# Token lists, gathers and weight chunks of a capacity-limited mixture of experts: moved token lists, moved gathers, a fourth raw buffer

## The chip, the cores and the metric

The kernel runs on one core of one Trainium2 chip, as one launch. The metric is the device time of one execution in microseconds (us). Engines are named as in the profile: PE (TensorE, matrix products), PEld (its weight loads), DVE (VectorE), ACT (ScalarE), POOL (GpSimd) and SP (SyncE, which here only issues DMAs).

## The reference, cut to what matters

```python
x = attention(q, k, v)                    # 4 batches, 8 heads, 576 positions; local and strided masks
x = x.reshape(2304, 512)
h = x @ w_in; x = maximum(0.01 * h, h) @ w_out          # 512 -> 2048 -> 512
logits = x @ w_gate                                     # 2304 tokens, 8 experts
order = argsort(-logits.flatten())
for idx in order:                                       # greedy: best pairs first
    tok, e = idx // 8, idx % 8
    if assigned[tok] >= 0 or counts[e] >= 288: continue
    assigned[tok] = e; counts[e] += 1
for e in range(8):                                      # 288 tokens each
    mask = assigned == e
    out[mask] = maximum(x[mask] @ w1[e], 0) @ w2[e]     # 512 -> 1024 -> 512
```

## The kernel before, in words

The program has three stages. Attention and most of the two-layer network `w_in`, `w_out` come first; the last two of six token blocks of that network have their second product done in `second(4)` and `second(5)` (lines 887 to 904), which write the tokens `x` to a DRAM buffer `x2d`. The change begins there. Then come the eight experts, in the order in which they fill up.

**Finding the experts.** `routes()` (lines 906 to 909) is a generator that goes round eight times. Round k has `search()`, which finds the next expert to be full and its threshold by five counting rounds: DVE builds 0/1 tiles `G` by comparisons, PE counts with them (`cnt`), DVE makes a flag, PE sums it (`tot`), and each needs the one before. `route(k)` then writes the number of the expert (`EXP[k]`, tile `ei`), a running count of its tokens by a scan and two small products (`po`), and strikes the chosen tokens and the expert out of the table `L`, `unl`, `opn`. `tokens(k)` turns the running count `s` into the list of the expert's 288 tokens: ten small DVE operations, three comparisons `OQ`, two tiles `rhs`, 18 products `pi`, and the list `idx` as whole numbers (`IDX[k]`). Only after that does the next search begin in the order of the program. `m`, `s`, `cc` and the other small state lie in one PSUM tile, `st`. DVE operations of this part are called through `soon` (line 641), which places them 2000 positions earlier in the planner's order.

**One expert.** `weights(k)` reads `EXP[k]` on SP and loads the expert's weights in eight chunks of 512 KB into three buffers `raw`: chunks 0 to 3 are `w1`, 4 to 7 are `w2`. ACT rounds each to `whi`; the rest `wlo = raw - whi` is taken by DVE for chunks 1, 5, 7 and by POOL for the other five; then the `raw` buffer is free again. There are two sets of `w1` tiles, but five buffers for the four chunks of `w2`, so that chunks 5 to 7 of the next expert can be rounded only when the last products of the running one have let go of theirs. `gather(k)` fetches the expert's tokens from `x2d` by three indirect DMAs that POOL issues, into one of two buffers `xg`; PE transposes them (`pet`), ACT and DVE write them as `exh` and `exl`. `expert(k)` has 96 products of 288 columns to the hidden layer, with ACT's `hh` and DVE's `hl` after each group, and 96 to the output (`g`, line 859 to 861); PE transposes the result (`pot`), ACT copies it into `o` (two buffers), and three indirect DMAs of POOL scatter it. The last quarter and the scatter of an expert are put off (`left_`) into the second column of the next one.

**What sets the order.** The main loop (lines 934 to 951) interleaves these generators: `expert(k)` yields 32 times; at every second yield `routes()` makes a step; at the yield with number 3 `need(k + 1)` runs `routes()` until the next token list is there, and `weights(k + 1)` begins, a chunk at each even yield from 6 to 20; `gather(k + 1)` follows at yields 22 to 24. One round of `routes()` has 16 steps, ten in the search, two in `route`, four in `tokens`, and an expert gives 16. So route(k + 2) runs beside expert k.

Each engine executes its own instructions strictly in order. That order is fixed when the program is built: a list planner with its own estimates of durations takes, for each engine, the ready instruction that stands first in the program; `tc.high_priority(n)` moves instructions n positions forward. On the chip an instruction waits by semaphores for what it needs, and all behind it on its engine wait too.

Of the kernel before, what the change touches and what calls it, by code (L numbers as in the profile page):

```python
# [7 lines left out]
F32 = mybir.dt.float32  # L8
# [5 lines left out]
OP = mybir.AluOpType  # L14
# [4 lines left out]
DM, FF = 512, 2048  # L19
# [7 lines left out]
def body(ctx, tc, q, k, v, w_in, w_out, w_gate, w1, w2, out):  # L27
    nc = tc.nc
    consts = ctx.enter_context(tc.tile_pool(name="consts", bufs=1, reuse_waits="tile"))
    dram = ctx.enter_context(tc.tile_pool(name="dram", bufs=1, space=bass.MemoryType.DRAM))  # L30
    x2d = dram.tile([NT, DM], F32, name="x2d")
# [443 lines left out]
    for n, _ in enumerate(mlp()):  # L475
        st = n // 7
# [47 lines left out]
    for n in range(64, 96):  # L524
# [22 lines left out]
        if f % 4 == 0:  # L547
            x = "hl"[f // 4 % 2]
# [8 lines left out]
        if f % 4 == 2 and f > 3 or f == 15:  # L557
            c = f // 4 - (f < 15)
# [69 lines left out]
    def rtile(shape, name, dt=F32, bufs=2):  # L628
        return rt.tile(shape, dt, name=name, tag=name, bufs=bufs)
# [5 lines left out]
    IDX, EXP = {}, {}  # L635
# [76 lines left out]
    def route(k):  # L712
        if k < 7:
            ab = yield from search()
        else:
            ab = rtile([128, 2, 18], "ab")
            soon.tensor_copy(ab[:, 0], unl)
            soon.memset(ab[:, 1], 0.0)
            soon.tensor_copy(oh, opn)
        ev = rtile([128, 1], "ev")  # L720
        t8 = rtile([128, 8], "t8")
        soon.scalar_tensor_tensor(t8, oh, 1.0, jf[:, :8], op0=OP.mult, op1=OP.mult, accum_out=ev)
        EXP[k] = rtile([128, 1], "ei", I32, bufs=8)
        soon.tensor_copy(EXP[k], ev)

        soon.tensor_tensor_scan(sc.rearrange("p a i -> p (a i)"), rst.rearrange("p a i -> p (a i)"),
                                     ab.rearrange("p a i -> p (a i)"), 0.0, op0=OP.mult, op1=OP.add)
        tot = rtile([128, 2], "tot", BF)
        soon.tensor_copy(tot, sc[:, :, 17])
        for _ in range(2):  # L730
            yield
        po = rbank([128, 2], "po")
        nc.tensor.matmul(po, tri, tot, start=True, stop=False)
        nc.tensor.matmul(po[:, 1:2], onesb, tot[:, 0:1], start=False, stop=True)
        s1 = rtile([128, 18], "s1")
        soon.scalar_tensor_tensor(s1, sc[:, 1], po[:, 1:2], ab[:, 1], op0=OP.add, op1=OP.mult)
        soon.scalar_tensor_tensor(s, sc[:, 0], po[:, 0:1], ab[:, 0], op0=OP.add, op1=OP.mult)
        soon.tensor_add(s, s, s1)
        if k < 7:
            t = rtile([128, 18], "t18")  # L740
            soon.tensor_scalar(t, s, 0.5, None, op0=OP.is_ge)
            soon.scalar_tensor_tensor(sel, s, 288.5, t, op0=OP.is_le, op1=OP.mult)
            soon.scalar_tensor_tensor(L, bc(sel, 8), -1.0e38, L, op0=OP.mult, op1=OP.add)
            soon.scalar_tensor_tensor(L, bc8(oh), -1.0e38, L, op0=OP.mult, op1=OP.add)
            soon.tensor_sub(unl, unl, sel)
            soon.tensor_sub(opn, opn, oh)
        yield from tokens(k)

    def tokens(k):

        c1 = rtile([128, 2, 18], "c1")
        soon.tensor_scalar(c1[:, 0], s, 96.5, None, op0=OP.is_ge)
        soon.tensor_scalar(c1[:, 1], s, 192.5, None, op0=OP.is_ge)
        soon.scalar_tensor_tensor(s, c1[:, 0], -96.0, s, op0=OP.mult, op1=OP.add)
        soon.scalar_tensor_tensor(s, c1[:, 1], -96.0, s, op0=OP.mult, op1=OP.add)
        soon.tensor_scalar(cc[:, 0], c1[:, 0], -1.0, 1.0, op0=OP.mult, op1=OP.add)
        soon.tensor_copy(cc[:, 2], c1[:, 1])
        soon.tensor_sub(cc[:, 1], c1[:, 0], cc[:, 2])
        soon.tensor_scalar(s, s, -1.0, None, op0=OP.add)
        OQ = rtile([128, 18, 96], "OQ", BF, bufs=1)  # L760
        for i in range(0, 18, 6):
            soon.tensor_tensor(OQ[:, i:i + 6], jf[:, None, :96].to_broadcast([128, 6, 96]),
                               s[:, i:i + 6].unsqueeze(2).to_broadcast([128, 6, 96]), op=OP.is_equal)
        rhs = rtile([128, 2, 3, 18], "rhs", BF)
        soon.tensor_mul(rhs[:, 0], cc, jf[:, None, :18].to_broadcast([128, 3, 18]))
        soon.tensor_scalar(rhs[:, 1], cc, tokp, None, op0=OP.mult)
        for _ in range(4):
            yield
        pi = rbank([96, 2, 3], "pi")
        for i in range(18):  # L770
            nc.tensor.matmul(pi.rearrange("p t c -> p (t c)"), OQ[:, i], rhs[:, :, :, i].rearrange("p t c -> p (t c)"),
                             start=(i == 0), stop=(i == 17))
        ip = rtile([96, 2, 3], "ip")
        soon.tensor_copy(ip, pi)
        IDX[k] = rtile([96, 3], "idx", I32, bufs=8)
        soon.scalar_tensor_tensor(IDX[k], ip[:, 0], 128.0, ip[:, 1], op0=OP.mult, op1=OP.add)
# [3 lines left out]
    def ind(ap):  # L780
        return bass.IndirectOffsetOnAxis(ap=ap, axis=0)

    def weights(k):
        e = nc.values_load(EXP[k][0:1, 0:1], engines=[mybir.EngineType.SP], min_val=0, max_val=7)
        W[k] = []
        for n in range(8):
            raw = POOLA[0].tile([128, 1024], F32, name="raw", tag="raw", bufs=3)
            if n < 4:
                nc.sync.dma_start(raw, w1[bass.ds(e, 1), 128 * n:128 * n + 128, :].rearrange("e p m -> (e p) m"))
            else:  # L790
                nc.sync.dma_start(raw.rearrange("p (j m) -> p j m", j=2),
                                  w2[bass.ds(e, 1), 256 * (n - 4):256 * (n - 4) + 256, :].rearrange(
                                      "e (j p) m -> p (e j) m", j=2))
            if n < 4 and k % 2:
                hi, lo = (xa.tile([128, 1024], F32R, name="w" + x, tag=f"WI{n + y}") for x, y in (("hi", 0), ("lo", 4)))
            else:
                pool, tag, bufs = (POOLB[0], "w2", 5) if n >= 4 else (POOLA[0], "w1", 4)
                hi = pool.tile([128, 1024], F32R, name="whi", tag=tag + "h", bufs=bufs)
                lo = pool.tile([128, 1024], F32R, name="wlo", tag=tag + "l", bufs=bufs)
            nc.scalar.activation(hi, raw, AF.Copy)  # L800
            (nc.vector if n in (1, 5, 7) else nc.gpsimd).tensor_sub(lo, raw, hi.bitcast(F32))  # L801
            W[k].append((hi, lo))
            yield

    def gather(k):
        xg = xa.tile([96, 3, DM], F32, name="xg", tag=("xh2", "xl2")[k % 2])
        for c in range(3):
            with tc.high_priority(2000):
                nc.gpsimd.indirect_dma_start(out=xg[:, c], out_offset=None, in_=x2d[:, :],
                                             in_offset=ind(IDX[k][:, c:c + 1]))  # L810
        if k % 2:
            xh, xl = (xa.tile([128, 4, 288], F32R, name="ex" + x, tag=f"x{x}3") for x in "hl")
        else:
# [13 lines left out]
    def expert(k):  # L827
# [4 lines left out]
        for j in range(8):  # L832
# [9 lines left out]
                left_.pop()()  # L842
            nc.scalar.activation(hh[:, j], p, AF.Relu)  # L843
            nc.vector.scalar_tensor_tensor(hl[:, j], p, 0.0, hh[:, j].bitcast(F32), op0=OP.max, op1=OP.subtract)
        o = e2.tile([96, 3, DM], F32, name="o", tag="o", bufs=2)

        def back(c, ot):
            pt = bank([96, 3, 128], "pot", "m")
# [19 lines left out]

        def end():
            back(3, ots[3])  # L870
            put()

        def put():
            for r in range(3):
                st = nc.gpsimd.indirect_dma_start(out=out, out_offset=ind(IDX[k][:, r:r + 1]), in_=o[:, r],
                                                  in_offset=None)
                for x in scat:
                    tc.declare_no_dep(st.ins, x.ins, reason="each token has one expert and one place")
                scat.append(st)
        if k < 7:  # L880
            left_.append(end)
        else:
# [21 lines left out]
            yield  # L904

    def routes():
        for k in range(8):
            yield from route(k)
            ROUTED[0] = k + 1

    ROUTED = [0]
    R = routes()

    def need(k):
        while ROUTED[0] <= k:
            next(R, None)

    for _ in second(4):
        next(R, None)
    gdx.close()  # L920
    POOLA[0] = ctx.enter_context(tc.tile_pool(name="pa", bufs=1, reuse_waits="tile"))
    need(0)
    wx = weights(0)
    for f, _ in enumerate(second(5)):
        next(R, None)
# [1 line left out]
            next(wx)  # L927
    right.close()
    POOLB[0] = ctx.enter_context(tc.tile_pool(name="pbx", bufs=1, reuse_waits="tile", side="right"))
    for _ in gather(0):  # L930
        pass
    for _ in wx:
        pass
    for k in range(8):
        nxt = iter(())
        for n, _ in enumerate(expert(k)):
            if n % 2 == 0:
                next(R, None)
            if n == 3 and k < 7:
                need(k + 1)  # L940
                wx = weights(k + 1)
            if n >= 6 and n % 2 == 0:
                next(wx, None)
            if n == 22 and k < 7:
                nxt = gather(k + 1)
                next(nxt)
            if n >= 22:
                next(nxt, None)
        for x in (wx, nxt):
            for _ in x:  # L950
                pass

# [29 lines left out]
```

## Time and profile before

| | |
|---|---|
| median of 3 runs | 925.15 us (921.23 to 933.21) |
| the profiled execution | 926.83 us |
| its span, first to last instruction | 925.1 us |
| mean granted TensorE clock | 0.963 |
| PE busy, share of the span | 860.2 us, 93% |
| DVE, ACT, POOL busy | 563.3, 441.9, 471.5 us |
| first product of expert 0, start of its last | 627.7 and 662.6 us |
| starts of experts 1 to 7 | 662.9, 697.1, 734.7, 773.1, 815.0, 856.6, 885.6 us |

Times within an execution are counted from the span's start. An instruction of PE is pipelined: one of 288 columns shows as 0.29 us busy, while the next begins 0.13 us after it, so that a wait on PE shows as a gap only when it is longer than the overlap.

### The profile page before, as it was taken

Reading aid. Unit: us, or ns where it says so; the run is one execution under the profiler, and the core shown is the slowest. Engines: PE = TensorE matmul, PEld = TensorE weight load, DVE = VectorE, ACT = ScalarE, POOL = GpSimd, SP = SyncE. Lnnn points to the kernel's source line nnn. Section 1 sums busy time; section 2 is a strip of 40 time slices with the busy share of each in tenths; the row PEclk is TensorE's granted clock in tenths of the full one; section 3 lists DMA queues with packets and bytes.
Section 4 is the critical chain, followed back from the end, with each engine's and each line's share of the span. In section 5 each row is a group of like instructions: output and inputs, shape, how many; then the busy total and the mean of one; then the engine's idle time right before and its main releaser. Section 6 shows DMA issues by size and latency. Waiting matters only on the chain.

```text
span 925.1 us, 16905 instructions
## 1 busy us (share of the span) xinstructions
PE 860.2 (93%) x6274; PEld 726.1 (78%) x6274; DVE 563.3 (61%) x1543; ACT 441.9 (48%) x1095; POOL 471.5 (51%) x394
## 2 busy tenths in 40 slices
PE   7889998899999999999999999978998989897994
PEld 4777766587887888778898877658998989797994
DVE  6777889856446445554555556566877767675330
ACT  5778667464446445454455423324435434243531
POOL 3645646564555556555655445745446263426621
PEclk9789999999999999999999999987999999798997
DMA  8596554320111100100000002325356362425710
GB/s 183 142 200 157 141 144 124 119 61 5 36 26 53 43 14 2 47 1 1 35 1 1 1 1 80 114 67 177 129 154 185 102 182 95 141 92 154 213 35 26
DMA packets 86450, 80.59 MB, mean 87 GB/s; under 512 B 65376, under 2 KB 65376, under 8 KB 86368
## 3 DMA queue, kind: packets, MB, share of 16 engines
q1 hardware_dynamic: 78688, 53.30, 21.1%
q0 software_dynamic: 7680, 26.22, 9.3%
q8 instruction: 49, 0.80, 0.4%
q14 instruction: 33, 0.27, 0.1%
HBM read 70.06 MB, written 9.44 MB: 86 GB/s over the span
## 4 chain that ended last, share of the span: by engine, by line
PE 64%; DMA 10%; DVE 9%; issue 7%; POOL 4%; ACT 4%; SPq 1%; POOLq 0%; ACTq 0%; DVEq 0%
PE p L373 5%; PE p L397 5%; DMA raw<-in_moe_w_dram 4%; PE p L375 4%; PE p L374 4%; PE p L399 4%; PE p L398 4%; PE g L859 3%; PE g L860 3%; PE g L861 3%; PE p L536 2%; PE q L896 2%; PE p L538 2%; PE pS L166 2%; PE p L537 2%
## 5 line engine op out<-in xcount | busy, mean ns | idle before, releaser
L352 POOL TENSOR_TENSOR lo<-WO,hi 128x512 fp32r<-128x512 f32 x96 | 126.6, 1319 | 95.1 <-ACT hi L349 94.9
L352 POOL TENSOR_TENSOR lo<-WI,hi 128x512 fp32r<-128x512 f32 x96 | 126.9, 1323 | 90.1 <-DVE hi L351 58.3
L801 POOL TENSOR_TENSOR wlo<-raw,whi 128x1024 fp32r<-128x1024 f32 x40 | 95.8, 2410 | 113.9 <-ACT whi L800 113.3
L373 PE MATMUL p<-xh,hi 128*128 128x384 f32 x256 | 98.1, 383 | 5.5 <-DVE g L382 5.5
L349 ACT ACTIVATE hi<-WO 128x512 fp32r<-128x512 f32 x96 | 60.5, 630 | 88.2 <-PE q L898 43.7
L375 PE MATMUL p<-xh,lo 128*128 128x384 f32 x256 | 86.9, 339 | 1.4 <-POOL lo L352 1.4
L800 ACT ACTIVATE whi<-raw 128x1024 fp32r<-128x1024 f32 x64 | 66.1, 1055 | 44.4 <-DMA raw<-in_moe_w_dram 39.2
L374 PE MATMUL p<-xl,hi 128*128 128x384 f32 x256 | 86.6, 338 | 0.6 <-DVE xl L234 0.6
L397 PE MATMUL p<-hi,gh 128*128 128x512 f32 x192 | 82.8, 431 | 0.8 <-ACT gh L383 0.8
L859 PE MATMUL g<-hh,whi 128*128 128x288 f32 x256 | 81.4, 319 | 0.5 <-ACT hh L843 0.5
L860 PE MATMUL g<-hl,whi 128*128 128x288 f32 x256 | 79.0, 309 | 0.1
L861 PE MATMUL g<-hh,wlo 128*128 128x288 f32 x256 | 78.7, 307 | 0.0
L836 PE MATMUL g<-exh,whi 128*128 128x288 f32 x256 | 78.4, 307 | 0.0
L837 PE MATMUL g<-exl,whi 128*128 128x288 f32 x256 | 77.4, 303 | 0.0
L838 PE MATMUL g<-exh,wlo 128*128 128x288 f32 x256 | 77.2, 302 | 0.0
L399 PE MATMUL p<-hi,gl 128*128 128x512 f32 x192 | 75.7, 394 | 1.3 <-DVE gl L384 1.3
L159 ACT ACTIVATE sc<-sc,mx 96x128 f32<-96x128 f32 (+2 forms) x176 | 67.6, 386 | 16.6 <-DVE mx L157 16.6
L398 PE MATMUL p<-lo,gh 128*128 128x512 f32 x192 | 75.2, 392 | 0.0
L373 PEld LDWEIGHTS p<-xh,hi 128*128 128x128 f32 x256 | 48.2, 188 | 16.6 <-DVE g L382 6.8
L181 POOL TENSOR_TENSOR sc<-sc,mx 96x384 f32<-96x384 f32 (+2 forms) x64 | 52.3, 834 | 17.3 <-DVE mx L179 10.2
L381 ACT ACTIVATE g<-p 128x384 f32<-128x384 f32 x64 | 31.1, 486 | 57.0 <-PE p L375 56.7
L351 DVE CAST hi<-WI 128x512 fp32r<-128x512 f32 x59 | 26.8, 454 | 46.1 <-PE p L374 35.9
(203 smaller groups left out, 2257.5 us busy)
## 6 DMA issues: line engine op xcount, KB each, us to landing
raw<-in_moe_w_dram SPq DMA_DIRECT2D x64, 512.0 KB
wraw<-in_moe_w_in_dram POOLq DMA_DIRECT2D x16, 512.0 KB
wraw<-in_moe_w_out_dram POOLq DMA_DIRECT2D x16, 512.0 KB
rawq<-in_q_dram SPq DMA_DIRECT2D x32, 144.0 KB
rawk<-in_k_dram SPq DMA_DIRECT2D x32, 144.0 KB
x2d<-x SPq DMA_DIRECT2D x18, 256.0 KB
vt<-in_v_dram SPq DMA_DIRECT2D x16, 160.0 KB
vt<-in_v_dram SPq DMA_DIRECT2D x48, 27.0 KB
```

The costliest lines, as they stand in the source:

```text
L352: nc.gpsimd.tensor_sub(lo, src, hi.bitcast(F32))
L373: nc.tensor.matmul(p1, wh[:, cs], xh[:, c], start=(c == 0), stop=False)
L374: nc.tensor.matmul(p1, wh[:, cs], xl[:, c], start=False, stop=False)
L375: nc.tensor.matmul(p1, wl[:, cs], xh[:, c], start=False, stop=(c == 3))
L397: nc.tensor.matmul(p2[t], gh[:, s], oh, start=(f == 0), stop=False)
L398: nc.tensor.matmul(p2[t], gh[:, s], ol, start=False, stop=False)
L399: nc.tensor.matmul(p2[t], gl[:, s], oh, start=False, stop=(f == 15))
L801: (nc.vector if n in (1, 5, 7) else nc.gpsimd).tensor_sub(lo, raw, hi.bitcast(F32))
L836: nc.tensor.matmul(p, wh, xh[:, c], start=(c == 0), stop=False)
L859: nc.tensor.matmul(p, wh, hh[:, j], start=(j == 0), stop=False)
L860: nc.tensor.matmul(p, wh, hl[:, j], start=False, stop=False)
L861: nc.tensor.matmul(p, wl, hh[:, j], start=False, stop=(j == 7))
```

## The change

- `route(k)` no longer runs `tokens(k)`. `routes()` keeps it as a generator `T` and makes one of its steps (seven now: the small operations, `OQ` and `rhs` are spread over them) beside each step of the search of round k + 1. Two counters, `FOUND` (the expert's number is known) and `LISTED` (its token list is there), take the place of `ROUTED`. A round of `routes()` has 12 steps then instead of 16, still 16 to an expert.
- `weights`: four `raw` buffers, not three; `wlo` of chunk 1 on POOL as well, so that six of eight are POOL's. `o` has one buffer, not two.
- The main loop waits for `FOUND` at yield 3, makes chunks 0 to 4 at yields 4 to 12, waits for `LISTED` at yield 16, issues the three gathers there, transposes at yields 24, 26, 28 and 30, and makes chunks 5 to 7 after the expert's last yield.
- The indirect DMAs of `gather` lose their `high_priority(2000)`, except that all of `gather(0)`, transposes included, gets 4000.

```diff
-        yield from tokens(k)
 
     def tokens(k):
...
+        yield
         soon.scalar_tensor_tensor(s, c1[:, 1], -96.0, s, op0=OP.mult, op1=OP.add)
+        soon.tensor_scalar(s, s, -1.0, None, op0=OP.add)
         soon.tensor_scalar(cc[:, 0], c1[:, 0], -1.0, 1.0, op0=OP.mult, op1=OP.add)
         soon.tensor_copy(cc[:, 2], c1[:, 1])
-        soon.tensor_sub(cc[:, 1], c1[:, 0], cc[:, 2])
-        soon.tensor_scalar(s, s, -1.0, None, op0=OP.add)
+        yield
...
         for i in range(0, 18, 6):
             soon.tensor_tensor(OQ[:, i:i + 6], ...)
+            yield
+        soon.tensor_sub(cc[:, 1], c1[:, 0], cc[:, 2])
...
-        for _ in range(4):
-            yield
+        yield
         pi = rbank([96, 2, 3], "pi")
...
+        yield
         ip = rtile([96, 2, 3], "ip")
...
-            raw = POOLA[0].tile([128, 1024], F32, name="raw", tag="raw", bufs=3)
+            raw = POOLA[0].tile([128, 1024], F32, name="raw", tag="raw", bufs=4)
...
-            (nc.vector if n in (1, 5, 7) else nc.gpsimd).tensor_sub(lo, raw, hi.bitcast(F32))
+            (nc.vector if n in (5, 7) else nc.gpsimd).tensor_sub(lo, raw, hi.bitcast(F32))
...
         for c in range(3):
-            with tc.high_priority(2000):
-                nc.gpsimd.indirect_dma_start(out=xg[:, c], ...)
+            nc.gpsimd.indirect_dma_start(out=xg[:, c], ...)
+        yield
...
-        o = e2.tile([96, 3, DM], F32, name="o", tag="o", bufs=2)
+        o = e2.tile([96, 3, DM], F32, name="o", tag="o")
...
     def routes():
+        T = iter(())
         for k in range(8):
-            yield from route(k)
-            ROUTED[0] = k + 1
+            if k == 7:
+                for _ in T:
+                    yield
+            for _ in route(k):
+                if k and next(T, 1) == 1:
+                    LISTED[0] = k
+                yield
+            for _ in T:
+                yield
+            LISTED[0] = k
+            FOUND[0] = k + 1
+            T = tokens(k)
+        for _ in T:
+            yield
+        LISTED[0] = 8
...
-    for _ in gather(0):
-        pass
+    need(LISTED, 0)
+    with tc.high_priority(4000):
+        for _ in gather(0):
+            pass
...
-            if n == 3 and k < 7:
-                need(k + 1)
-                wx = weights(k + 1)
-            if n >= 6 and n % 2 == 0:
-                next(wx, None)
-            if n == 22 and k < 7:
-                nxt = gather(k + 1)
-                next(nxt)
-            if n >= 22:
-                next(nxt, None)
-        for x in (wx, nxt):
+            if k < 7:
+                if n == 3:
+                    need(FOUND, k + 1)
+                    wx = weights(k + 1)
+                if 4 <= n < 14 and n % 2 == 0:
+                    next(wx)
+                if n == 16:
+                    need(LISTED, k + 1)
+                    nxt = gather(k + 1)
+                    next(nxt)
+                if n >= 24 and n % 2 == 0:
+                    next(nxt, None)
+        for x in (nxt, wx):
```

## Rows read from the trace of the kernel before

**Rows 1.** Windows by expert: length; PE, PEld, DVE, ACT, POOL busy; clock; DMA.

```profile
628.00:663.00 35.00, 34.46 (x292) 33.38 (x291) 25.82 (x70) 15.81 (x29) 13.25 (x6) 0.90 0.44 136
663.00:697.00 34.00, 33.17 (x315) 31.26 (x314) 25.84 (x68) 14.69 (x28) 17.55 (x12) 1.00 0.50 159
697.00:734.70 37.70, 34.60 (x337) 32.62 (x334) 27.97 (x69) 15.88 (x29) 17.69 (x12) 1.00 0.48 144
734.70:773.00 38.30, 35.45 (x332) 33.59 (x330) 27.24 (x68) 16.01 (x29) 18.52 (x12) 0.96 0.48 142
773.00:815.00 42.00, 37.30 (x307) 35.29 (x304) 27.77 (x74) 15.90 (x28) 17.21 (x12) 0.88 0.40 130
815.00:856.50 41.50, 34.86 (x288) 33.45 (x286) 27.52 (x85) 15.14 (x28) 19.58 (x15) 0.92 0.47 141
856.50:885.50 29.00, 28.42 (x218) 27.95 (x217) 10.13 (x15) 15.02 (x29) 15.74 (x9) 1.00 0.57 172
885.50:917.00 31.50, 27.76 (x211) 27.22 (x208) 6.24 (x9) 8.08 (x20) 7.03 (x7) 0.97 0.09 26
```

**Rows 2.** Waits of PE, 628 to 893: total us, times, longest.

```profile
PE pet L819 <- DMA xg<-x2d,idx: 7.1, 2, 4.2
PE cnt L683 <- DVE G L641: 4.5, 4, 2.4
PE pi L771 <- DVE rhs L641: 3.3, 4, 1.6
PE po L733 <- DVE tot L641: 1.4, 2, 1.3
```

**Rows 3.** Timeline of PE: start, us, instruction, idle time before it and releaser.

```profile
626.34 0.16 PE L690 MATMUL tot<-f,units 64*128 64x1 bf16 x1 [2.80 <-issue]
...
799.76 1.56 PE L819 MATMUL pet<-ident,xg 96*128 96x96 f32 x4 [2.92 <-DMA xg<-x2d,idx]
...
844.81 0.74 PE L819 MATMUL pet<-ident,xg 96*128 96x96 f32 x3 [4.21 <-DMA xg<-x2d,idx]
845.34 0.85 PE L850 MATMUL pot<-ident,ot 128*96 128x128 f32 x3
```

**Rows 4.** Timeline of DVE in the round that finds expert 5.

```profile
780.48 0.16 DVE L641 TENSOR_TENSOR opn<-opn,st 128x8 f32<-128x8 f32 x1
...
784.54 0.46 DVE L844 SCALAR_TENSOR_TENSOR hl<-g,hh 128x288 fp32r<-128x288 f32 x1 [2.42 <-ACT hh L843]
...
788.56 0.30 DVE L641 TENSOR_REDUCE st<-L 128x18 f32<-128x144 f32 x1
...
788.99 1.91 DVE L641 SCALAR_TENSOR_TENSOR idx<-ip 96x3 int32<-96x3 f32 x1
```

**Rows 5.** Waits of SP's queue, 628 to 893.

```profile
SPq L791 <- POOL wlo L801: 73.8, 22, 12.7
SPq L784 <- DVE st L641: 68.7, 6, 25.9
```

**Rows 6.** Waits of ACT, 628 to 893.

```profile
ACT whi L800 <- DMA raw<-in_moe_w_dram: 39.0, 26, 3.9
```

**Rows 7.** Waits of DVE, 628 to 893.

```profile
DVE hl L844 <- ACT hh L843: 26.6, 22, 3.0
```

**Rows 8.** Groups on POOL, 628 to 893: count, busy us, mean ns, idle before.

```profile
L801 POOL TENSOR_TENSOR wlo<-raw,whi 128x1024 fp32r<-128x1024 f32 x36 | 86.3, 2412 | 113.5 <-ACT whi L800 112.9 <-issue 0.5
```

**Rows 9.** Groups on DVE, the same stretch.

```profile
L801 DVE TENSOR_TENSOR wlo<-raw,whi 128x1024 fp32r<-128x1024 f32 x23 | 39.2, 1705 | 11.6 <-ACT whi L800 11.6
```

**Rows 10.** Line 801, whole span: ns shortest, median, longest; first and last start.

```profile
L801 DVE TENSOR_TENSOR wlo<-raw,whi x24: 1206/1226/3317, 582.9 to 886.1; 128x1024 fp32r<-128x1024 f32 x24
```

**Rows 11.** Timeline of POOL about expert 5's gather and expert 4's scatter.

```profile
794.32 0.93 POOL L809 DMA_INDIRECT xg<-x2d,idx  x1 [0.16 <-issue]
...
823.44 0.92 POOL L875 DMA_INDIRECT out_dram<-o,idx  x1 [0.30 <-issue]
```

More of the change, by code (lines that the diff above doesn't have):

```diff
@@ L807, in gather @@
         for c in range(3):
-            with tc.high_priority(2000):
-                nc.gpsimd.indirect_dma_start(out=xg[:, c], out_offset=None, in_=x2d[:, :],
-                                             in_offset=ind(IDX[k][:, c:c + 1]))
+            nc.gpsimd.indirect_dma_start(out=xg[:, c], out_offset=None, in_=x2d[:, :],
+                                         in_offset=ind(IDX[k][:, c:c + 1]))
+        yield
         if k % 2:
@@ L844, in expert, with put @@
             nc.vector.scalar_tensor_tensor(hl[:, j], p, 0.0, hh[:, j].bitcast(F32), op0=OP.max, op1=OP.subtract)
-        o = e2.tile([96, 3, DM], F32, name="o", tag="o", bufs=2)
+        o = e2.tile([96, 3, DM], F32, name="o", tag="o")
+        def put(r):
+            st = nc.gpsimd.indirect_dma_start(out=out, out_offset=ind(IDX[k][:, r:r + 1]), in_=o[:, r],
+                                              in_offset=None)
+            for x in scat:
+                tc.declare_no_dep(st.ins, x.ins, reason="each token has one expert and one place")
+            scat.append(st)
         def back(c, ot):
@@ L870, in end @@
             back(3, ots[3])
-            put()
-        def put():
             for r in range(3):
[L875 to L879, printed above, removed]
+                put(r)
         if k < 7:
@@ L906, in routes, with need @@
     def routes():
+        T = iter(())
         for k in range(8):
-            yield from route(k)
-            ROUTED[0] = k + 1
-    ROUTED = [0]
+            if k == 7:
[13 more added lines that the diff above has]
+        LISTED[0] = 8
+    FOUND, LISTED = [0], [0]
     R = routes()
-    def need(k):
-        while ROUTED[0] <= k:
+    def need(what, k):
+        while what[0] <= k:
             next(R, None)
@@ L921, in body @@
     POOLA[0] = ctx.enter_context(tc.tile_pool(name="pa", bufs=1, reuse_waits="tile"))
-    need(0)
+    need(FOUND, 0)
     wx = weights(0)
```

## Prediction, made before the changed kernel was run

> **What bounds the kernel now.** I read the windows by expert first [rows 1]. Everything that the diff moves belongs to the last third of the run, and there PE is nearly always busy: 33 to 37 us of each of the first six experts. But the experts aren't equally long. The last two, beside which no search runs, take 29.0 and 31.5 us with the tail; those with a search take 34.0 to 42.0. PE's own busy time differs less, so what differs is waiting: 42.0 - 37.3 = 4.7 us without PE in expert 4 and 41.5 - 34.9 = 6.6 in expert 5, against 0.8 in expert 1. In these two the granted clock is also low, 0.88 and 0.92.
>
> What PE waits for is in its waits [rows 2]: twice for a gather, 7.1 us, and for the search and its token lists (`cnt`, `pi`, `po`), 4.5 + 3.3 + 1.4 = 9.2 us. The two gathers have their places at 799.76 and 844.81, 2.92 and 4.21 us long [rows 3]: PE stands in the middle of an expert's second half, in front of transposes of the **next** expert's tokens.
>
> Why those tokens are late is seen on DVE [rows 4]. The list for expert 5 is finished at 788.99 + 1.91 = 790.90, 18 us after expert 4 began (773.1), and the gather is issued behind a weight subtraction at 794.32 [rows 11]. Search and token list are one chain, and it no longer keeps up with the experts. A good part of the chain is the token list: from the end of the bookkeeping, 780.64, to the first operation of the next search, 788.56, are 7.9 us. Of these 2.42 us are not work: DVE stands behind `hl`, which waits for ACT's `hh`. ACT in turn waits 39.0 us in all for `raw` to land [rows 6], and DVE 26.6 us for `hh` [rows 7]; a transfer that is late holds the search through two in-order engines. SP issues the weights late for two reasons: 68.7 us of waits for the expert's number, and 73.8 us in the `w2` line alone for POOL's subtraction to free a buffer [rows 5].
>
> So three things set the end: PE's own work, the search chain that sets when numbers and lists are there, and weight chunks that delay the chain.
>
> **The change part by part**, against the profiled execution (926.83 us, span 925.1); the median of the runs is 1.7 us lower, so the sum is lowered by that at the end.
>
> A. **Gathers in time.** The next search no longer waits for the list, which takes some of 7.9 us off the chain in each of the rounds before expert 6. In the program's order the numbers run further ahead, too: 12 steps to a round against 16 given per expert is a lead of four steps more with each expert. List and gather of expert 5 and 6 should be there long before yield 24. That takes 7.1 us off PE [rows 2] and some of the slow clock behind the two gaps: experts 4 and 5 lack (1 - 0.88) x 42.0 + (1 - 0.92) x 41.5 = 8.4 us of clock [rows 1], of which much lies in the idle time itself; I take 3. Bounds 0 (PE finds another late operand in the same places) and -15.5; I take **-10**, the row of the gaps with part of the clock, since those tokens lose the cause of their lateness, not only some of it.
>
> B. **Search waits.** 9.2 us of PE's waits are for DVE in the search and the list. `pi` has no successor in the search any more, and DVE is rid of eight subtractions with a mean of 1.705 us [rows 9], 13.6 us. On the other hand the planner puts each count at the very moment at which it believes `G` to be ready, so every delay that it doesn't know of is still a gap on PE. Bounds 0 and -9.2, and up to 3 us of clock more; I take **-6**, nearer to the gain, because the 2.42 us in [rows 4] show whose delay it is, and the next part eases that.
>
> C. **Fourth raw buffer.** Now the three transfers of chunks 5 to 7 sit in all buffers until the running expert ends; with a fourth, chunk 0 of the expert after it can be there. Its effect on PE goes through ACT and DVE and is in B; by itself 0, bounds +1 (more transfers at once, each longer) and -3.
>
> D. **Expert 0.** At 626.34 a `tot` holds PE 2.80 us while transposes of expert 0 are queued behind it [rows 3]. With 4000 positions these come in front of it. But the tokens themselves arrive only a little earlier, so **-1**, bounds 0 and -2.8.
>
> E. **Subtractions on POOL.** Eight more of 2.412 us [rows 8], 19.3 us of POOL. Cover: POOL stands 113.5 us in front of its subtractions waiting for ACT [rows 8], and is busy 17.2 to 19.6 us of an expert's 34 to 42 [rows 1], so about 21 of 33 afterwards. One of the eight falls in `second(5)`, where PE needs POOL's `lo` each step: there up to 2.4 us. If the cover were gone, all 19.3. **+1**, bounds 0 and +19.3. DVE's subtraction takes 1.206 us at the least, 3.317 at the most, mean 1.705 [rows 9, 10]. The Trainium skill (SBUF — State Buffer, section "SBUF: two separate sides") says that a DVE operation with two inputs in SBUF and a POOL operation take the second port in turn, each holding it for its whole length. The long ones in rows 10 agree with that. By this rule alone the sixteen subtractions left to DVE could all become as long as the longest, 16 x (3.317 - 1.705) = 25.8 us more against the 13.6 taken off; B would then be nothing and the time 917. I don't go by it, since POOL's added work falls mostly into its idle time, beside other operations of DVE than these.
>
> F. **Transposes later.** The last of them moves from yield 24 to 30, six groups of products closer to their first use; chunks 5 to 7 (ACT, 39.0 us of waits in rows 6 for such roundings) may come in front of the copy. I have no row for it. An upper bound is one such wait of mean 39.0 / 26 = 1.5 us at each of seven boundaries, 10.5; below nothing it can't be, for the transposes were not late in experts 0 to 3. I take **+1.5**: the planner now puts the copies ahead of those chunks.
>
> One `o` buffer costs nothing: the scatter of expert 4 is issued by 823.44 + 0.92 [rows 11], and expert 5 has its first transposed result at 845.34 [rows 3], 21 us later. If the scatter came that late, PE would stand. The three gathers without priority wait behind at most two subtractions, 4.8 us, and are needed eight yields later, about 7 us.
>
> Sum: -10 - 6 + 0 - 1 + 1 + 1.5 = **-14.5**. 926.8 - 14.5 = 912.3 for the profiled execution, 910.6 by the median: **911 us**, its own range 904 to 919.
>
> **Rivals.**
> 1. *PE keeps the whole gain.* All waits in rows 2 go (16.3 us), 8 us of clock and 2.8 of D: 925.15 - 27.1 = 898. For it: without searches experts take 29 us, and a search that is ahead delays nobody. Against: counts are still placed without slack.
> 2. *The waits come back elsewhere.* The planner sees the earlier lists, packs the counts as tightly as now, and PE waits at the boundaries for `exh` (F, up to 10.5) what it saved at the gathers. Or the change doesn't do what it says: already now the next search begins at 788.56, before `idx` at 788.99 [rows 4], so part of the list is overlapped, and DVE does the same sum of work. 925.15 - 10 + 8 = 923.
> 3. *POOL takes over (slower).* All five early chunks go through POOL one by one, 5 x 2.412 = 12.1 us, plus six indirect DMAs of 0.92 us and their pauses, before a buffer is free, a transfer lands and ACT can go on to `hh`. From the point at which POOL, not SP's wait for the number, ends last in front of every load, the eight extra subtractions count in full: 925.15 + 19.3 = 944. For it: 73.8 us of waits of SP for POOL [rows 5]. Against: a fourth buffer takes one subtraction out of this loop, and POOL's 113.5 idle us. The Trainium skill (GPSIMD Engine Reference, section "4.1 Engine selection") has elementwise work with two inputs on VectorE and calls POOL about twice as slow there. The rows agree on the price, 2.412 against 1.206 to 1.705; whether it is paid is what this rival and E differ in.
>
> **How the numbers follow.** Forecast 0.45, rival 1 0.27, rival 2 0.20, rival 3 0.08. About 2%, 18.5 us, is what a measurement of this kernel tells from no change: below 906.6 it is faster, above 943.7 slower. Rival 1 lies below 906.6, and of the forecast's range of 15 us the lowest 2.6, a sixth: 0.27 + 0.08 = 0.35 faster; 0.08 slower; 0.57 within. The range leaves out rival 3 and the lower tail of rival 1 (all waits and all clock, 890): 893 to 932.
>
> **What would show it.** A: no wait of `pet` for `xg` above 1 us in experts 4 and 5, each `idx` finished before its expert's predecessor begins, and these two experts under 34 us. B: `cnt` and `pi` waits under half of 9.2; the next search's first reduction within 2 us of `opn`. C: SP's waits for the number (68.7 us) nearly gone, ACT's for `raw` well below 39. D: no gap at `tot` in front of expert 0's transposes. E: POOL's busy time 19 us up with PE's waits for `lo` unchanged. F: waits of PE for `exh` or `exl` at the starts of experts. The prediction is wrong if counts still wait as long as now (rival 2), or if ACT's waits for `raw` grow because POOL frees the buffers later (rival 3).

## The result and the profile after

The changed kernel takes 940.0 us (median of 9 runs), the kernel before 926.81 us in the runs beside it: a ratio of 1.0131, 95% interval 1.0088 to 1.0174. It is 1.3% slower, less than the 2% that I had named as the size of a clear difference, but the interval leaves out 1, and I had forecast a gain of 1.5%; 940.0 us lies outside both ranges of the prediction. The profiled execution of after took 938.33 us, its span is 936.5 us. The level of the kernel before differs between the series of runs below (medians 917.8 to 928.7 us), so I compare ratios to the runs of before in the same series, not times.

The windows of after, one per expert, with the columns of [rows 1]:

```profile
629.00:671.40 42.40, 38.65 (x309) 36.99 (x309) 26.45 (x77) 17.34 (x32) 25.12 (x14) 0.84 0.51 152
671.40:708.50 37.10, 35.17 (x316) 33.17 (x315) 28.31 (x78) 15.77 (x28) 19.54 (x11) 0.95 0.45 148
708.50:749.40 40.90, 35.81 (x334) 33.74 (x333) 31.37 (x79) 15.66 (x29) 20.70 (x12) 0.96 0.42 131
749.40:789.50 40.10, 35.82 (x334) 33.74 (x333) 31.29 (x79) 15.31 (x29) 20.70 (x12) 0.96 0.42 136
789.50:826.90 37.40, 33.98 (x297) 32.72 (x296) 25.08 (x82) 12.42 (x25) 22.92 (x15) 0.95 0.49 159
826.90:862.90 36.00, 31.10 (x219) 30.22 (x218) 11.51 (x15) 16.52 (x31) 23.02 (x13) 0.93 0.47 150
862.90:895.50 32.60, 30.68 (x219) 30.37 (x217) 10.53 (x16) 14.15 (x27) 10.81 (x7) 0.92 0.30 100
895.50:928.00 32.50, 27.86 (x209) 27.08 (x207) 6.62 (x10) 8.03 (x21) 6.26 (x6) 1.00 0.08 25
```

Against [rows 1] experts 4 and 5 are 10.1 us shorter (37.4 and 36.0 for 42.0 and 41.5): the gain that I had written down for the gathers is there, net of whatever else befell these two. But experts 0 to 3 are 15.5 us longer together, expert 0 alone 7.4, and expert 6 is 3.6 us longer. So something has been added in nearly every expert. Only half of the 15.5 us is PE standing idle: its time without work in experts 0 to 3 rose from 7.3 to 15.0 us, and its busy time from 137.7 to 145.5 us. The longer busy time goes with a lower granted clock (0.84, 0.95, 0.96 and 0.96, where before had 0.90, 1.00, 1.00 and 0.96). After the two longest gaps of PE, 3.85 us up to 716.80 and 3.86 us up to 757.84, it is 0.50 from 718.0 to 721.4 us and 0.51 from 758.9 to 762.4, the lower of its two levels.

PE's waits of after, 628 to 893, as in [rows 2]:

```profile
PE cnt L683 <- DVE G L641: 14.7, 8, 3.9
PE g L839 <- DVE exl L824: 3.6, 2, 1.9
PE pet L821 <- ACT ot L876: 3.2, 1, 3.2
...
PE pi L772 <- DVE rhs L641: 0.4, 2, 0.2
...
PE pet L821 <- DMA xg<-x2d,idx: 0.2, 1, 0.2
```

The waits for gathers are gone (7.1 us, now 0.2), those of `pi` as well (3.3, now 0.4). The counts wait three times as long for DVE (4.5, now 14.7), and PE waits for ACT's `ot`, which it didn't do before. ACT, DVE and SP in the same stretch show behind whom, one fence each:

```profile
ACT whi L802 <- DMA raw<-in_moe_w_dram: 78.9, 31, 6.4
```

```profile
DVE exl L824 <- ACT exh L823: 35.6, 17, 7.3
```

```profile
SPq L791 <- POOL wlo L803: 79.6, 24, 9.1
SPq L791 <- DMA raw<-in_moe_w_dram: 55.8, 17, 4.3
...
SPq L786 <- DVE st L641: 12.4, 3, 6.1
```

SP hardly waits for the expert's number any more (68.7 us, now 12.4), as forecast. It waits for buffers and for transfers in the `w1` line instead. And ACT waits 78.9 us for `raw` to land, where it was 39.0 [rows 6]; I had forecast "well below 39". Both signs by which the prediction was to be wrong have come: the counts wait longer, and so does ACT for `raw`; the reason named there for the second, POOL, is weighed below.

What this looks like is in the chain of waits of after, in expert 0's second half; start, length, what:

```profile
641.59 4.78 POOL wlo L803 x2
...
646.38 4.37 DMA raw<-in_moe_w_dram
...
650.77 1.07 ACT whi L802
...
651.91 2.41 POOL wlo L803
...
654.33 3.51 DMA raw<-in_moe_w_dram
...
658.83 0.46 ACT o L860
659.29 0.31 ACT exh L823
...
659.62 0.46 DVE exl L824
660.08 1.33 DVE G L641
...
661.46 0.73 PE cnt L683 x18
```

A buffer is freed by POOL, its load takes 4.37 us, ACT rounds, POOL subtracts, the same buffer is loaded again. Three buffers hold chunks 5 to 7 of expert 1, which can't be rounded before the last products of expert 0 let go of their tiles; the fourth takes the `w1` chunks of expert 2 one after another, since its number is known by now. And ACT has its `whi` of each ahead of `o`, `exh` and `ot` in its queue. ACT's own timeline, with the idle time in front:

```profile
644.00 0.41 ACT L845 ACTIVATE hh<-g 128x288 fp32r<-128x288 f32 x1 [0.54 <-PE g L840]
650.77 1.06 ACT L802 ACTIVATE whi<-raw 128x1024 fp32r<-128x1024 f32 x1 [6.36 <-DMA raw<-in_moe_w_dram]
651.74 0.39 ACT L876 ACTIVATE ot<-g 128x288 f32<-128x288 f32 x1
654.76 0.41 ACT L876 ACTIVATE ot<-g 128x288 f32<-128x288 f32 x1 [2.64 <-PE g L870]
657.87 1.06 ACT L802 ACTIVATE whi<-raw 128x1024 fp32r<-128x1024 f32 x1 [2.69 <-DMA raw<-in_moe_w_dram]
658.83 0.46 ACT L860 COPY o<-pot 96x384 f32<-96x384 f32 x1
```

That gave **theory 1**: ACT, in order, stands in front of landings in the second half of each expert; the early number and the fourth buffer together make this possible. The rivals were **theory 2**, POOL's eight added subtractions, and **theory 3**, the list's operations spread through the search, which would hold up DVE.

### The profile page after: what moved, and what is told of

It reads as the page before. It is cut to its first block, busy times and chain, and to the rows that moved or that the text cites. A ratio compares the mean times of both kernels' runs of the same rounds, so it can differ in the third digit from the quotient of the medians.

```text
span 936.5 us, 16919 instructions
## 1 busy us (share of the span) xinstructions
PE 866.5 (93%) x6274; PEld 732.2 (78%) x6274; DVE 562.1 (60%) x1535; ACT 441.0 (47%) x1095; POOL 494.3 (53%) x402
## 4 chain that ended last, share of the span: by engine, by line
PE 59%; issue 11%; DVE 8%; DMA 8%; POOL 7%; ACT 5%; SPq 1%; POOLq 0%; ACTq 0%; DVEq 0%
PE p L373 5%; PE p L397 5%; POOL wlo L803 5%; DMA raw<-in_moe_w_dram 4%; PE p L375 4%; PE p L374 4%; PE p L399 4%; PE p L398 4%; PE p L536 2%; PE pS L166 2%; PE p L538 2%; PE p L537 2%; PE q L899 2%; PE q L900 2%; PE q L901 2%
## 5 line engine op out<-in xcount | busy, mean ns | idle before, releaser
L803 POOL TENSOR_TENSOR wlo<-raw,whi 128x1024 fp32r<-128x1024 f32 x48 | 116.2, 2430 | 107.0 <-ACT whi L802 100.5
L839 PE MATMUL g<-exl,whi 128*128 128x288 f32 x256 | 81.1, 317 | 4.9 <-DVE exl L824 4.9
L838 PE MATMUL g<-exh,whi 128*128 128x288 f32 x256 | 82.0, 322 | 0.0
L840 PE MATMUL g<-exh,wlo 128*128 128x288 f32 x256 | 80.1, 314 | 0.0
L839 PEld LDWEIGHTS g<-exl,whi 128*128 128x128 f32 x256 | 52.6, 206 | 5.9 <-DVE exl L824 5.8
```

Of the source, the lines that this page charges most:

```text
L803: (nc.vector if n in (5, 7) else nc.gpsimd).tensor_sub(lo, raw, hi.bitcast(F32))
L838: nc.tensor.matmul(p, wh, xh[:, c], start=(c == 0), stop=False)
L839: nc.tensor.matmul(p, wh, xl[:, c], start=False, stop=False)
L840: nc.tensor.matmul(p, wl, xh[:, c], start=False, stop=(c == 3))
```

## The experiments

**e1: the changed kernel with three raw buffers.**

```diff
-            raw = POOLA[0].tile([128, 1024], F32, name="raw", tag="raw", bufs=4)
+            raw = POOLA[0].tile([128, 1024], F32, name="raw", tag="raw", bufs=3)
```

> The changed kernel with three raw buffers again, all else as changed. Theory 1 (the fourth buffer lets one chunk of the expert after next circulate while chunks 5 to 7 hold the other three; ACT stands in front of each landing and DVE and PE behind it): ACT's waits for raw fall from 78.9 us in the expert stage to about 40, PE's waits for G from 14.7 to under 8, and the time falls to 912 to 925. Theory 2 (POOL's eight added subtractions are the cost): no change, 936 to 944. Theory 3 (the list's operations between the search's steps hold up DVE): no change, 936 to 944.

Measured: 923.15 us, ratio 0.9966 (0.9929 to 1.0003). ACT's waits for `raw`, 628 to 893:

```profile
ACT whi L802 <- DMA raw<-in_moe_w_dram: 36.2, 23, 3.9
```

The loss is gone with the buffer, as theory 1 said, but PE's waits for `G` only fell to 8.6 us, and the kernel isn't faster than before.

**e2: the changed kernel, chunk 1 subtracted on DVE again.**

```diff
-            (nc.vector if n in (5, 7) else nc.gpsimd).tensor_sub(lo, raw, hi.bitcast(F32))
+            (nc.vector if n in (1, 5, 7) else nc.gpsimd).tensor_sub(lo, raw, hi.bitcast(F32))
```

> The changed kernel with the subtraction of chunk 1 on DVE again (three of eight on DVE). Theory 1: within 6 us of the changed kernel, 934 to 944, ACT's waits for raw still above 65 us. Theory 2: most of the 13 us comes back, 922 to 930. Theory 3: slower than the changed kernel, since DVE has more to do.

Measured: 935.35 us, ratio 1.0114 (1.0047 to 1.0182), within the interval of the changed kernel. Theory 2 falls as the main cause. ACT's waits for `raw` were 51.4 us, lower than I expected of theory 1 (above 65).

**e3: the changed kernel, rounding held.** The edge orders ACT's instructions alone: the rounding of chunks 0 to 4 stands in ACT's queue behind an `hh` of the expert beside which the program has it. A buffer, though, stays full until its chunk is rounded.

```diff
+    LAST = [None]
+
     def weights(k):
...
-            nc.scalar.activation(hi, raw, AF.Copy)
+            with (tc.issue_after(LAST[0]) if LAST[0] is not None and n < 5 else ExitStack()):
+                nc.scalar.activation(hi, raw, AF.Copy)
...
-            nc.scalar.activation(hh[:, j], p, AF.Relu)
+            LAST[0] = nc.scalar.activation(hh[:, j], p, AF.Relu).ins
```

> The changed kernel, but ACT's rounding of chunks 0 to 4 is queued behind the hh that was traced last (order of issue on ACT alone), so that none of them can stand in the second half of the expert before; loads and buffers as changed. Theory 1 in its narrow form (it is ACT standing in order in front of landings in the second half): ACT's waits for raw fall to 45 or less, gains of the earlier lists stay, 905 to 918. Theory 2: 936 to 944. Theory 3: 936 to 944. If the loads themselves were the cost (more transfers at once), the time stays above 930.

Measured: 911.71 us, ratio 0.9876 (0.9785 to 0.9966). The same two views as of after, ACT's wait and its timeline in expert 0's second half:

```profile
ACT whi L805 <- DMA raw<-in_moe_w_dram: 2.6, 4, 0.7
```

```profile
643.50 0.41 ACT L848 ACTIVATE hh<-g 128x288 fp32r<-128x288 f32 x1 [0.71 <-PE g L843]
649.08 0.41 ACT L879 ACTIVATE ot<-g 128x288 f32<-128x288 f32 x1 [5.17 <-PE g L873]
652.02 0.41 ACT L879 ACTIVATE ot<-g 128x288 f32<-128x288 f32 x1 [2.53 <-PE g L873]
652.35 0.48 ACT L863 COPY o<-pot 96x384 f32<-96x384 f32 x1
653.69 0.40 ACT L826 CAST exh<-pet 128x288 fp32r<-128x288 f32 x1 [0.87 <-PE pet L824]
```

No `whi` stands between `hh` and `ot`, and what ACT waits for is PE, as it should be. But the hold moves loads too. In after, SP issues the four `w1` chunks of expert 2 at 646.38 and 654.33, as the chain above has them, and then

```profile
661.39 0.33 SPq L791 DMA_DIRECT2D raw<-in_moe_w_dram  x1
...
669.71 0.33 SPq L791 DMA_DIRECT2D raw<-in_moe_w_dram  x1
```

one for each round of the buffer. In e3 the first lies where it lay, and the other three come only when chunks 5 to 7 let go of their buffers:

```profile
647.08 0.34 SPq L793 DMA_DIRECT2D raw<-in_moe_w_dram  x1
...
665.59 0.92 SPq L793 DMA_DIRECT2D raw<-in_moe_w_dram  x2
...
668.42 0.33 SPq L793 DMA_DIRECT2D raw<-in_moe_w_dram  x1
```

So e3 takes away the early roundings and the early loads behind the first together, and it can't tell them apart: that the time fell below 930 doesn't rule out the loads, as I had expected of it. It shows that the early load of the first chunk does no harm, and that the loss is in the early roundings and what circulates behind them. Against the loads as a cost of their own stand two rows of after: PE's waits for a transfer are 0.2 us from 628 to 893, and the DMA engines are not busier in experts 0 to 3 than before (0.51, 0.45, 0.42 and 0.42 of the time, where before had 0.44, 0.50, 0.48 and 0.48). That PE stands behind ACT's queue is seen in e9.

**e4: the kernel before with the token lists alone.** The diff of the change to `route`, `tokens` and `routes` with `FOUND` and `LISTED`; three raw buffers, gathers, chunks and subtractions as before.

> The kernel before with one part of the change alone: token lists built between the steps of the next search (weights may start when the number is known, gathers when the list is there, three raw buffers, DVE and POOL as before). Theory 1: the gathers are in time, with no circulating chunk: PE's waits for xg vanish (7.1 us before), 908 to 920. Theory 2: the same. Theory 3: 935 to 945.

Measured: 917.49 us, ratio 0.9901 (0.9865 to 0.9937). PE has no wait for `xg` in its list any more. Theory 3 falls: this part is a gain of 1%.

**e5: e3 with three raw buffers** (the edits of e1 and e3).

> The kernel of e3 (rounding of chunks 0 to 4 held behind the running expert's hh) with three raw buffers. If the fourth buffer is worth something once ACT doesn't stand in front of it (it has chunk 0 landed ahead): ACT's waits for raw rise from 2.6 us to about 30 and the time to 916 to 924. If order alone is what counts and the buffer nothing: 909 to 914, as e3.

Measured: 928.80 us, ratio 1.0029 (0.9987 to 1.0072), ACT's waits for `raw` 35.7 us. The time is above both ranges that I had expected. The fourth buffer, worth 1.65% of loss between e1 and the changed kernel, is worth 1.5% of gain once rounding is held. Neither half of e3 helps alone.

**e6: e3 with chunk 1 on DVE** (the edits of e2 and e3).

> The kernel of e3 with the subtraction of chunk 1 on DVE again. If POOL's added subtractions cost by themselves: faster than e3, 902 to 908. If they are covered, or spare DVE: 911 to 918.

Measured: 909.04 us, ratio 0.9824 (0.9745 to 0.9903), between the two expected ranges. Not to be told from e3: POOL's sixth subtraction has no price that these runs resolve.

**e7: e3 with earlier transposes.**

```diff
-                if n >= 24 and n % 2 == 0:
+                if n >= 20 and n % 2 == 0:
                     next(nxt, None)
```

> The kernel of e3 with the transposes of the gathered tokens at yields 20 to 26 in place of 24 to 30. If the late transposes cost what PE's waits for exl at the starts of three experts say (5.1 us in e3): those waits vanish and the time falls by 3 to 6 us, 905 to 909. If something else takes their place: 910 to 914.

Measured: 905.62 us, ratio 0.9776 (0.9696 to 0.9856). PE's waits in e3 began with this line:

```profile
PE g L842 <- DVE exl L827: 5.1, 3, 2.4
```

In e7 there is none of that kind, and no other in its place except one wait for `hl` that e3 has as well (3.3 there):

```profile
PE g L872 <- DVE hl L849: 4.1, 1, 4.1
```

By ratio e7 is 1.0% below e3, though their intervals overlap.

**e8: the kernel before with the held rounding alone** (the edit of e3).

> The kernel before with only the held rounding of e3, nothing of the change. If the hold is a gain of its own, whatever the rest: 912 to 920. If it pays only where chunks have landed ahead (fourth buffer and early number), and repairs what the change brought: within 1% of before, 920 to 934, ACT's waits for raw still above 30 us.

Measured: 931.47 us, ratio 1.0062 (1.0023 to 1.0100): by itself no gain but a small loss. ACT's waits for `raw` were 26.0 us, where I had expected more than 30.

**e9: e4 with the fourth raw buffer.** The edit of the buffer, and one `o` buffer.

> The kernel of e4 (token lists alone) with the fourth raw buffer (and one o buffer); gathers, DVE's three subtractions and the main loop as before. Theory 1 says that early number and fourth buffer together are the loss: ACT's waits for raw rise from 30.9 us in e4 to above 60, and the time from 917 to 930 or more. If the loss needed the moved gathers and chunks or POOL's sixth subtraction too: 912 to 922.

Measured: 930.38 us, ratio 1.0106 (1.0020 to 1.0192), 2% above e4, with intervals apart. ACT's waits for `raw` are back:

```profile
ACT whi L802 <- DMA raw<-in_moe_w_dram: 69.8, 21, 6.9
```

Here PE waits for ACT directly, 13.7 us in three lines of which e4 has none; the first is

```profile
PE g L861 <- ACT ot L869: 8.9, 3, 4.3
```

PE's longest wait of these, first on ACT and then on PE:

```profile
690.19 1.06 ACT L802 ACTIVATE whi<-raw 128x1024 fp32r<-128x1024 f32 x1 [5.66 <-DMA raw<-in_moe_w_dram]
691.16 0.98 ACT L823 CAST exh<-pet 128x288 fp32r<-128x288 f32 x3
692.01 0.43 ACT L869 ACTIVATE ot<-g 128x288 f32<-128x288 f32 x1
```

```profile
692.50 0.61 PE L861 MATMUL g<-hh,whi 128*128 128x288 f32 x1 [4.29 <-ACT ot L869]
```

ACT waits 5.66 us for a chunk, rounds it, and only then makes three `exh` and the `ot` for which PE has stood 4.29 us. Early number and fourth buffer are enough for the loss, and this is theory 1 in the trace.

**e10: the kernel before with the fourth raw buffer alone.**

> The kernel before with the fourth raw buffer alone (and one o buffer). Theory 1: the number is known late (68.7 us of SP's waits for it), so the fourth buffer has little to circulate: 918 to 932, ACT's waits for raw 35 to 50. If the buffer is the loss by itself: 934 or more.

Measured: 924.38 us, ratio 1.0033 (1.0000 to 1.0067); ACT's waits 22.1 us, where I had expected 35 to 50. SP's waits suggest why the buffer does little harm here, the number comes too late for it to circulate:

```profile
SPq L784 <- DVE st L641: 96.5, 6, 31.3
```

**e11: e7 with chunk 1 on DVE.**

> The kernel of e7 (held rounding, transposes at yields 20 to 26) with the subtraction of chunk 1 on DVE again. If e6's 2.7 us and e7's 6 us add up: 900 to 905. If they don't: 905 to 909.

Measured: 898.03 us, ratio 0.9770 (0.9699 to 0.9840). The time is below both expected ranges, but before is faster in this series too (922.52 us); by ratio it is the same as e7, so the two gains are not seen to add up. It is a version faster than both kernels, by 2.3% against before.

**e12: the kernel before with six of eight subtractions on POOL.**

> The kernel before with six of eight subtractions on POOL, nothing else. If POOL's idle time covers them, as the prediction had it: 922 to 932. If each lengthens the loop of buffer, transfer and rounding: 932 to 944.

Measured: 919.05 us, ratio 0.9961 (0.9922 to 1.0001). The time is below the expected range with before's level; by ratio there is no cost.

**e13 and e14: all eight subtractions on POOL**, in the changed kernel and in e7. In after, the two longest waits of PE for `G` have another look than the chain above. DVE's timeline about the first:

```profile
710.08 5.34 DVE L803 TENSOR_TENSOR wlo<-raw,whi 128x1024 fp32r<-128x1024 f32 x1
715.34 1.41 DVE L641 SCALAR_TENSOR_TENSOR G<-th,tot,st 128x1152 bf16<-128x1152 f32 x1
716.67 1.21 DVE L803 TENSOR_TENSOR wlo<-raw,whi 128x1024 fp32r<-128x1024 f32 x1
```

and POOL's at that time:

```profile
709.61 4.71 POOL L803 TENSOR_TENSOR wlo<-raw,whi 128x1024 fp32r<-128x1024 f32 x2
```

DVE's subtraction takes 5.34 us instead of 1.21 and ends 1.1 us after POOL's pair does, about its own length. `G` is behind it, and PE's count starts at 716.80 after 3.85 us idle. Is that a cause of its own?

```diff
-            (nc.vector if n in (5, 7) else nc.gpsimd).tensor_sub(lo, raw, hi.bitcast(F32))
+            nc.gpsimd.tensor_sub(lo, raw, hi.bitcast(F32))
```

> The changed kernel with all eight subtractions on POOL, so that none of DVE's can be held by one of POOL's. If that hold is a cause of its own: the two 4 us gaps of PE vanish and the time falls by 6 to 10 us, 929 to 934, with ACT's waits for raw still above 60 us. If it is only what the waits of ACT look like on DVE: 936 to 944.

> The kernel of e7 (held rounding, transposes at yields 20 to 26) with all eight subtractions on POOL. If DVE's holds are a cause of their own that is still there in e7 (mean 1878 ns against 1206 alone, 14 of them, 9 us of DVE): 900 to 904. If POOL's queue becomes the limit (8 x 2.43 + 6 x 1.25 = 27 us of 34): 907 to 920.

Measured: e13 932.35 us, ratio 1.0143 (1.0067 to 1.0220); e14 905.08 us, ratio 0.9846 (0.9770 to 0.9921). In times e13 lies in the range that the hold was to show, but before is faster in this series (917.84 us), and by the ratio nothing came back; I go by the ratio. e14 lies between the two ranges that I had expected. The two gaps are gone, PE waits elsewhere, and ACT stands as long as ever, or longer:

```profile
ACT whi L802 <- DMA raw<-in_moe_w_dram: 87.5, 32, 7.6
```

So the hold decides where a gap shows, not how much is lost, as far as an interval of 0.8% to either side can tell.

## Why the prediction was wrong

- **A, gathers: right in kind.** Lists are done at 749.4 and 789.5 for experts 4 and 5, as experts 3 and 4 begin; the waits for `xg` are gone, and experts 4 and 5 are 10.1 us shorter for a forecast of 10. That the two figures agree is in part luck: what follows is in these experts too, and they didn't get under 34 us. e4, where the earlier lists stand alone, is at 0.9901.
- **C, the fourth buffer: this is the step that failed.** I had written that by itself it is 0, with +1 to -3, and had taken its effect on ACT for a relief: chunk 0 landed ahead. I saw that three buffers are held by chunks 5 to 7, and didn't ask what the planner does with the one that is left when the number is known 24 us and more before the expert begins in whose program part the chunks stand. It doesn't wait for that expert; it sends the chunks through the one buffer, and puts their roundings into ACT's queue in front of what PE needs. Measured: a loss of 2.05% between e4 and e9, of 1.65% between e1 and after. The buffer itself doesn't cost: with rounding held it gains 1.5% (e5 to e3).
- **B, search waits: wrong as a consequence.** The words were that DVE's delay is ACT's and that C eases it; instead C made it longer: 9.2 us of `cnt`, `pi` and `po` became 15.1 of `cnt` and `pi`. Of the 13.6 us that DVE was to be rid of, 2.6 came: over the whole span the 24 subtractions of before took 42.4 us, the 16 of after 39.8, each 2.487 us instead of 1.765. The rule of the Trainium skill (SBUF — State Buffer, section "SBUF: two separate sides"), which I had weighed and not gone by, described DVE's side better than I did; the longest took 5.34 us, where I had gone up to 3.317. The end it didn't move (e13).
- **D, expert 0: nothing.** The gap of 2.80 us at `tot` is gone, but counts wait 1.78 and 1.51 us in the same place, and expert 0 begins at 629.0 for 627.7.
- **E, POOL: right.** POOL's busy time rose by 22.8 us over the span; e2, e6 and e12 show no price for it. Rival 3, which would have been 944, came near in its time, and it had the loop right: POOL frees a buffer, a transfer lands, ACT goes on, and ACT's waits for `raw` grew as it said. It was wrong in the price: it counted the eight added subtractions, but without them (e2) the time didn't come back. My argument against it, that the fourth buffer takes one subtraction out of this loop, was wrong too: the buffer is what let the loop run early.
- **F, late transposes: right in kind, probably too small.** I took 1.5 us; in after PE waits 4.9 us for `exl` over the span, in e3 5.1, and e7 without them is 1.0% lower by ratio, with intervals that overlap.

C is not the whole miss. e1 is the change without the fourth buffer, to which the sum gave 0, and it is at 0.9966 where I had forecast 911 / 925.15 = 0.985. So of the 2.8% between forecast and result the buffer is 1.65%, and about 1.2% is missing from the other parts. The lists alone are worth 1% (e4); e1, which adds the moved gathers, transposes and chunks and the sixth subtraction, is 0.65% behind e4, with intervals that just overlap. The late transposes are the nearest candidate, and no run tests them there. That e3 comes so close to the forecast, at 0.9876, is luck: it has in it 1.5% from the fourth buffer that the sum didn't have.

Two things stay argued and not shown: how much of the loss is ACT's place in front of the loads and how much anything else that circulates with them, and that the planner puts the rounding there because its own load is shorter than the 4.37 us of the chip. The runs show where it puts it, that PE stands behind it, and what the fourth buffer costs.

## What to carry to other kernels

When data become known earlier or a buffer is added, look at what the planner will start with it, and on which in-order engine the first consumer of the load stands: a load that nobody needs yet can hold everything behind that consumer. Ask of each such instruction whether the engine's next urgent one could be queued in front; here an edge of order on ACT, which also kept three of each four early loads back, turned 1.3% of loss into 1.2% of gain. And a wait of an engine that is not the bottleneck (ACT, 39 us) is a row to follow to the bottleneck's queue, not to halve in one's head.

## What the runs showed of the hardware that was not expected

DVE's subtraction with both inputs in SBUF was held not through one but through two POOL subtractions in a row: 5.34 us at 710.08, while POOL ran two from 709.61 to 714.32; alone it took 1.21 us at 716.67. The same picture is at 751.11 (5.34 us). It isn't always so: at 793.24 DVE took 2.95 us beside two of POOL's, and POOL's pair 5.68 us instead of 4.71, so there DVE got its turn in between. The Trainium skill (SBUF — State Buffer, section "SBUF: two separate sides") says that the operation which comes first has the shared port pair for its whole length and the other blocks fully. The trace agrees that one waits for the other's end; at 710.08 and 751.11 the one that was blocked did not get its turn between two of POOL's.
